# Two-source VectorE operations for the mirrored copies of the first two blocks and for the first step's copy

## Chip, core and metric

The kernel runs on one core of a Trainium2 chip. The metric is the device time of one execution in microseconds (us), from three runs; beside them stands one execution that the hardware profiler recorded. TensorE (PE), VectorE (DVE), ScalarE (ACT) and GpSimd (POOL) compute; the queue of SyncE (SP) and that of ACT issue transfers.

## What is computed

The program is an attention with a complex decaying state, then two feed-forward layers. Only the first part is touched by the change:

```python
B, H, S, D = q.shape                               # 4, 8, 768, 48
mag = np.sqrt(a_re * a_re + a_im * a_im)
scale = np.minimum(mag, 0.999) / (mag + 1e-06)
a_re_n, a_im_n = (a_re * scale, a_im * scale)
for t in range(S):
    ar, ai = (a_re_n[:, :, t, :, None], a_im_n[:, :, t, :, None])
    new_re = ar * S_re - ai * S_im
    new_im = ar * S_im + ai * S_re
    kv = np.einsum('bhd,bhe->bhde', k[:, :, t], v[:, :, t])
    S_re, S_im = (new_re + kv, new_im)
    y[:, :, t] = np.einsum('bhd,bhde->bhe', q[:, :, t], S_re)
```

Behind it, each token goes through one of eight experts (`_moe_ref`) and then through a dense layer with a leaky ReLU (`_moe2_ref`).

## The kernel before

The sequence is cut into chunks of L = 96 steps. Within a chunk the products P of all a up to a step are needed, so that k can be divided and q multiplied by them; these are the rows that `attention_rows` makes. It is called twice, once for each half of the batch. The first call keeps the results in two large tiles called `stash`; the second writes them to memory. A row of its tiles is one of the 128 partitions: two batches, eight heads, eight chunks. The 96 steps are worked off in blocks (BLKA: 4 steps, then ten blocks of 8, then 6, 4 and 2).

For each block i there are these pieces:

- `load_a(i)` brings a_re and a_im of the block into a tile `ari` (three buffers), over the SP queue; `load_kq(i)` brings k and q.
- `norm_pre(i)` is ACT's part of the normalization: squares (`nsq`), logarithm, exponential (`nr`), square (`nrr`). The sum of the two squares is made by PE (`ad`) except in the first three blocks, where DVE makes it.
- `norm(i)` is DVE's part: three operations that end with the factor `rr` (named `nrr` in the rows), then a_re and a_im times `rr` into parts 0 and 2 of the tile `a4` (named `a`). Then parts 3 and 1 get the mirrored copies: part 3 is part 0, and part 1 is minus part 2. In most blocks ACT makes these; in blocks 0 and 1 (MIRROR) DVE does, and in the last ones (MIRROR_G) POOL makes one of them.
- `steps(i)` is the recurrence: for each step one multiplication of the last P with the four parts of a (`t<-P,a`) and one sum (`P<-t`). The first step of all has no last P; there P is a copy of parts 0 and 2.
- `scaled_pre(i)`, `scaled(i)` and `turned(i)` make k/P and q*P (`kr`, `qr`), turn them on PE (`qkps`) and copy them into `stash` on ACT.

In the first call the order of all these on DVE, ACT and PE is written out: `timed` gives every piece a place, and the three engines keep it. POOL and SP are filled in the order in which the program comes to them. Between the pieces stand those of `gate_products` (`gv`, `gtps`, `gps`), which work on v for the later gate. Ahead of the block work POOL is given its constants and, last, two memsets that clear partitions 96 to 127 of the two `stash` tiles (12288 elements each).

After this stage come the chunk products and the routing, then experts and dense layers of the first half, beside which the second call of `attention_rows` runs, and then the same for the second half.

Of the kernel before, what the change touches and what calls it, by code (L numbers as in the profile page):

```python
# [14 lines left out]
ALU = mybir.AluOpType  # L15
# [53 lines left out]
MIRROR = (0, 1)  # L69
# [9 lines left out]
def moe_attention_kernel(ctx, tc, q, k, v, a_re, a_im, w_skip, w_gate, w1, w2, w_in, w_out, out,  # L79
# [15 lines left out]
    V, A, T, G = Engine(nc.vector, "V"), Engine(nc.scalar, "A"), Engine(nc.tensor, "T"), Engine(nc.gpsimd, "G")  # L95
# [58 lines left out]
    def attention_rows(ui, ep, blks, sum_pe, queue, store, stash=None, more=None):  # L154
# [9 lines left out]
        nb = len(blks)  # L164
        tbm = max(blks)

        def rows(src, i):
            return src[b0:b0 + HB].rearrange("b h (c t) d -> c (b h) (t d)", t=L)[
                :, :, t0s[i] * D:(t0s[i] + blks[i]) * D]

        def flat(x):
            return x.rearrange("p t d -> p (t d)")

        def cost(i, n=1):
            return (70 + 1.04 * n * blks[i] * D) / 1e3

        def tl(tag, i, dims=(), after=(), bufs=None):
            kw = {} if bufs is None else {"bufs": bufs}
            t = ep.tile([R, *dims, tbm, *after, D], F32, tag=tag, name=tag, **kw)
            n = blks[i]  # L180
            return t[:, :, :n] if len(dims) == 1 else t[:, :n]

        def both(x, i):
            return x.unsqueeze(2).to_broadcast([R, blks[i], 2, D])
# [14 lines left out]
        def load_a(i):  # L199
            ari = tl("ari", i, (2,), bufs=3)  # L200
            queue.dma_start(flat(ari[:, 0]), rows(a_re, i))
            queue.dma_start(flat(ari[:, 1]), rows(a_im, i))
            ins["a", i] = ari
# [29 lines left out]
        def norm(i):  # L233
            ari = ins.pop(("a", i))
            m2, s2, r0, rr = pre["a", i]
            V.tensor_tensor(rr, m2, rr, ALU.mult)
            yield cost(i)
            V.scalar_tensor_tensor(rr, rr, 3.0, r0, ALU.subtract, ALU.mult)
            yield cost(i)
            V.scalar_tensor_tensor(rr, rr, -2.0, s2, ALU.max, ALU.mult)  # L240
            yield cost(i)
            a4 = tl("a4", i, (), (4,))
            a4s[i] = a4
            if stash:
                V.tensor_tensor(a4[:, :, 0, :], ari[:, 0], rr, ALU.mult)
                yield cost(i)
                V.tensor_tensor(a4[:, :, 2, :], ari[:, 1], rr, ALU.mult)
            else:
                V.tensor_tensor(a4[:, :, 0::2, :], ari.rearrange("p c t d -> p t c d"), both(rr, i), ALU.mult)
            if i + 3 < nb:  # L250
                load_a(i + 3)
            yield cost(i, 2)
            for _ in range(3 if ui else 0):
                yield 0.0
            for c in range(2):
                if stash and i in MIRROR_G and not c:
                    G.tensor_scalar(a4[:, :, 3 - 2 * c, :], a4[:, :, 2 * c, :], 1.0 - 2 * c, None, ALU.mult)
                elif stash and i in MIRROR:
                    V.tensor_scalar(a4[:, :, 3 - 2 * c, :], a4[:, :, 2 * c, :], 1.0 - 2 * c, None, ALU.mult)
                else:  # L260
                    A.activation(a4[:, :, 3 - 2 * c, :], a4[:, :, 2 * c, :], AF.Copy, scale=1.0 - 2 * c)

        def scaled_pre(i):
            P = Ps[i]
            sq = ep.tile([R, tbm, 2, D], F32, tag="psq", name="psq")[:, :blks[i]]
            g0 = tl("pg0", i)
            A.activation(sq, P, AF.Square)
            yield
            n2 = added(sq[:, :, 0, :], sq[:, :, 1, :], i, SUM_SCALED)
            yield  # L270
            s2 = sq[:, :, 1, :]
            A.activation(s2, n2, AF.Ln)
            yield
            A.activation(g0, s2, AF.Exp, scale=-1.0)
            pre["k", i] = n2, g0
# [59 lines left out]
        def steps(i, prev):  # L335
            a4 = a4s.pop(i)
            P = ep.tile([R, tbm, 2, D], F32, tag="P", name="P", bufs=3)[:, :blks[i]]
            Ps[i] = P
            for t in range(blks[i]):
                if prev is None:  # L340
                    V.tensor_copy(P[:, t], a4[:, t, 0::2, :])
                else:
                    t4 = ep.tile([R, 2, 2, D], F32, tag="t4", name="t4", bufs=3)
                    V.tensor_tensor(t4, prev.unsqueeze(1).to_broadcast([R, 2, 2, D]),
                                    a4[:, t].rearrange("p (o i) d -> p o i d", i=2), ALU.mult)
                    yield 0.33
                    V.tensor_tensor(P[:, t], t4[:, :, 0, :], t4[:, :, 1, :], ALU.add)
                prev = P[:, t]
                yield 0.23
# [22 lines left out]
        def timed(more):  # L372
# [18 lines left out]
            at(s0, 1, later(norm_pre, 0), (0, 1, 2, 3, 4))  # L391
            at(s0, 1, later(norm_pre, 1), (4.5, 7.2, 9.5, 10.5, 12.5))
            at(s0, 1, later(norm, 0), (5, 6, 7, 8, 8.5, 9))
            t = end = 0.0
            for i in range(nb + 1):
                t, n = end, max(2.0 * blks[min(i, nb - 1)], LEAST)
                end = t + n
                if i < nb:
                    at(t, 1, later(lambda i: steps(i, Ps[i - 1][:, blks[i - 1] - 1] if i else None), i),
                       range(2 * blks[i] - (i == 0)))  # L400
                if i == nb:
                    at(t, 1, lambda: chunk_products(), (0.5,))
                if i + 1 < nb:
                    at(t, n, later(norm, i + 1), AT_NORM)
                if i + 2 < nb:
                    at(t, n, later(norm_pre, i + 2), AT_NORM_PRE)
                if i:
                    at(t, n, later(scaled_pre, i - 1), AT_SCALED_PRE)
                    at(t, n, later(scaled, i - 1), AT_SCALED)
                if i > 1:  # L410
                    at(t, n, later(lambda i: turns.pop(0), i), AT_TURNED[:2 * -(-blks[i - 2] // 4)])
# [22 lines left out]
        for j in range(2):  # L434
            for _ in norm_pre(j):
                yield 0.4
            if not j:
                yield from norm(0)
        prev = None
        for i in range(nb):  # L440
            before = ([scaled_pre(i - 1)] if i else []) + ([norm_pre(i + 2)] if i + 2 < nb else [])
            others = ([(None, norm(i + 1))] if i + 1 < nb else []) + ([(("k", i - 1), scaled(i - 1))] if i else [])
            yield from weave(steps(i, prev), before, others)
            prev = Ps[i][:, blks[i] - 1]
# [735 lines left out]
    stash = [p.tile([128, NCH, HB * H, L], F32, name="stash") for p in blocks]  # L1180
    ep = tc.alloc_tile_pool(name="rows0", bufs=2, side="right")
    more = []
    gen = attention_rows(0, ep, BLKA, True, nc.sync, rws[0], stash, more)
    next(gen)
    constants()
# [12 lines left out]
    rt = tc.alloc_tile_pool(name="rt", bufs=1, side="right")  # L1198
    ck[0].take(1)
    behind = attention_rows(1, ep, BLKB, False, nc.sync, rws[1])  # L1200

    def place(e, layer):
# [237 lines left out]
```

## Time and profile before

| | us |
|---|---|
| median of three runs | 968.27 |
| lowest, highest | 965.54, 970.45 |
| the profiled execution | 965.6 |
| its span from the first to the last instruction | 963.3 |

Over the span PE is busy 87%, DVE 65%, ACT 54%, POOL 14%. The chain of work that ended last lies 52% on PE, 19% on DVE, 15% in transfers, 10% on ACT.

The stage of the change is the first 165 us. A busy instruction in these records is one that has been started; the time in which a started instruction is held up counts as its own duration. All kernel instructions carry line 91, that of the helper that records them, so they are told apart by the tiles they write and read. The names in the timeline: start in us, duration in us, engine, line, operation, out<-in, size.

### The profile page before, as it was taken

The numbers are of one execution on the slowest core, as the hardware profiler recorded it, in microseconds if no ns is written. First come the engines' busy times: TensorE is split into PE (matmuls) and PEld (weight loads), VectorE is DVE, ScalarE is ACT, GpSimd is POOL, SyncE is SP. The second block draws the span as 40 slices with busy tenths as digits, with TensorE's granted clock in tenths as the row PEclk, the third lists the DMA queues.
The fourth block names the chain that finished last, engine by engine and source line by source line (L and its number), as shares of the span: only waits on it lengthen the run. The fifth ranks groups of instructions, "written<-read, shape, count | busy, mean of one in ns | idle before, by whom it ended". The sixth has DMA issues, their size and how long they took to land.

```text
span 963.3 us, 17827 instructions
## 1 busy us (share of the span) xinstructions
PE 835.0 (87%) x6674; PEld 581.0 (60%) x6674; DVE 628.5 (65%) x1534; ACT 517.9 (54%) x1065; POOL 137.2 (14%) x168
## 2 busy tenths in 40 slices
PE   0488877899569975699999988999999999999997
PEld 0366666899458853344556978945677645546454
DVE  7998796477868678999990456487668262260440
ACT  2578898566445443564751777656557162250430
POOL 9100011212163001100002211141101000000000
PEclk9978798999879988799999999999999999999999
DMA  4265552798848985625436799332857201000000
GB/s 113 70 184 149 149 143 87 201 264 268 272 152 280 318 289 181 222 86 177 145 97 174 196 256 246 107 119 100 266 182 246 79 9 51 17 0 26 9 10 27
DMA packets 126512, 143.61 MB, mean 149 GB/s; under 512 B 34058, under 2 KB 109514, under 8 KB 126416
## 3 DMA queue, kind: packets, MB, share of 16 engines
q1 hardware_dynamic: 106064, 107.88, 38.2%
q10 hardware_dynamic: 18304, 29.89, 9.6%
q0 software_dynamic: 2048, 4.61, 1.4%
q8 instruction: 54, 0.88, 0.4%
q14 instruction: 42, 0.34, 0.1%
HBM read 115.62 MB, written 28.41 MB: 150 GB/s over the span
## 4 chain that ended last, share of the span: by engine, by line
PE 52%; DVE 19%; DMA 15%; ACT 10%; issue 3%; SPq 1%; POOL 0%; ACTq 0%; DVEq 0%; POOLq 0%
PE ops L91 17%; PE hps L91 13%; PE yps L91 7%; PE sps L91 3%; DVE gg L91 3%; DMA raw<-in_moe_w_in_dram 3%; DVE gl L91 3%; DVE cst L91 3%; ACT stash L91 2%; DVE a L91 2%; ACT gh L91 2%; DMA kqt<-kqd 2%; PE tps L91 2%; PE ad L91 2%; DMA vt<-vd 2%
## 5 line engine op out<-in xcount | busy, mean ns | idle before, releaser
L91 PE MATMUL hps<-xTh,m2w 128*128 128x512 f16 x576 | 173.7, 381 | 0.4 <-ACT xTh L91 0.2
L91 PEld LDWEIGHTS <-m2w 128*128 128x128 f16 x864 | 84.4, 98 | 100.3 <-issue 3.2
L91 PE MATMUL ops<-m2w,gh 128*128 128x384 f16 x512 | 125.2, 326 | 0.0
L91 PE MATMUL hps<-xTl,m2w 128*128 128x512 f16 x288 | 109.3, 380 | 0.2 <-DVE xTl L91 0.2
L91 DVE TENSOR_TENSOR gg<-hps,gg 128x512 f32<-128x512 f32 x96 | 65.8, 686 | 65.1 <-ACT gg L91 64.7
L91 PE MATMUL ops<-m2w,gl 128*128 128x384 f16 x256 | 83.6, 327 | 0.0
L91 ACT ACTIVATE ot<-ops 128x384 f32<-128x384 f32 x24 | 11.6, 489 | 121.3 <-PE ops L91 121.3
L91 PEld LDWEIGHTS <-gh 128*128 128x128 f16 x512 | 50.1, 98 | 32.7
L91 DVE TENSOR_TENSOR t<-P,a 128x192 f32<-128x192 f32 x190 | 67.1, 353 | 1.3 <-ACT a L91 0.4
L91 PE MATMUL ops<-m2w,stash 128*128 128x384 f16 x384 | 65.3, 326 | 1.2 <-ACT m2w L91 1.2
L91 DVE TENSOR_TENSOR gl<-gg,gh 128x512 f16<-128x512 f32 x64 | 44.2, 690 | 33.9 <-ACT gh L91 33.2
L91 ACT ACTIVATE gg<-hps 128x512 f32<-128x512 f32 x96 | 56.3, 587 | 17.4 <-PE hps L91 12.0
L91 DVE SCALAR_TENSOR_TENSOR w<-cw,w 128x768 f16<-128x768 f32 x64 | 59.8, 953 | 7.3 <-ACT w L91 7.1
L91 ACT ACTIVATE gh<-gg 128x512 f16<-128x512 f32 x64 | 40.3, 630 | 42.9 <-DVE gg L91 42.7
L91 ACT ACTIVATE w<-cw 128x768 f16<-128x768 f32 x64 | 53.0, 843 | 18.1 <-DMA cw<-in_moe_w_dram 15.7
L91 POOL TENSOR_SCALAR_AFFINE_SELECT sc<-sc 96x384 f32<-96x384 f32 x64 | 35.2, 559 | 156.2 <-ACT sc L91 156.0
L91 PE MATMUL ad<-psq,ident 128*128 128x384 f32 (+2 forms) x48 | 24.9, 657 | 36.8 <-ACT psq L91 36.2
L91 PEld LDWEIGHTS <-stash 128*128 128x128 f16 x384 | 37.5, 98 | 28.6 <-issue 4.3
L91 POOL DMA_INDIRECT xd<-xo,idx x16 | 25.2, 1575 | 179.6 <-DVE xo L91 165.8
L91 ACT ACTIVATE stash<-qkps 96x512 f32<-96x512 f32 (+1 forms) x50 | 50.1, 1026 | 0.3 <-PE qkps L91 0.3
L91 DVE TENSOR_TENSOR P<-t 128x96 f32<-128x96 f32 x190 | 48.1, 253 | 1.6
L91 PE MATMUL yps<-stash,hh 128*128 128x384 f32 x128 | 44.7, 503 | 3.5 <-ACT hh L91 3.5
(245 smaller groups left out, 1786.1 us busy)
## 6 DMA issues: line engine op xcount, KB each, us to landing
stash<-in_moe_w_dram ACTq DMA_DIRECT2D x32, 768.0 KB
cw<-in_moe_w_dram SPq DMA_DIRECT2D x64, 384.0 KB
kqt<-kqd SPq DMA_DIRECT2D x16, 576.0 KB
kqd<-kq SPq DMA_DIRECT2D x14, 576.0 KB
vd<-gv SPq DMA_DIRECT2D x32, 192.0 KB
vt<-vd SPq DMA_DIRECT2D x32, 192.0 KB
raw<-in_moe_w_in_dram SPq DMA_DIRECT2D x16, 384.0 KB
raw<-in_moe_w_out_dram SPq DMA_DIRECT2D x16, 384.0 KB
```

The costliest lines, as they stand in the source:

```text
L91: ins = getattr(self.engine, op)(*args, **kw)
```

## The change

Three edits:

1. In blocks 0 and 1 the mirrored copies are no longer made from parts 0 and 2 by an operation with one source tensor and a constant (`tensor_scalar`), but from `ari` and `rr`, as parts 0 and 2 themselves, by an operation with two source tensors and a constant (`scalar_tensor_tensor`): (a times plus or minus 1) times rr.
2. The first step's P is no longer a copy but the maximum of the same view with itself (`tensor_tensor` with max), again two source operands.
3. Since the mirrored copies now read `ari`, in these two blocks `load_a(i + 3)`, which takes over that buffer, is issued behind them.

```diff
-            if i + 3 < nb:
+            if i + 3 < nb and not (stash and i in MIRROR):
                 load_a(i + 3)
             yield cost(i, 2)
...
                 elif stash and i in MIRROR:
-                    V.tensor_scalar(a4[:, :, 3 - 2 * c, :], a4[:, :, 2 * c, :], 1.0 - 2 * c, None, ALU.mult)
+                    V.scalar_tensor_tensor(a4[:, :, 3 - 2 * c, :], ari[:, c], 1.0 - 2 * c, rr, ALU.mult, ALU.mult)
                 else:
                     A.activation(a4[:, :, 3 - 2 * c, :], a4[:, :, 2 * c, :], AF.Copy, scale=1.0 - 2 * c)
+            if i + 3 < nb and stash and i in MIRROR:
+                load_a(i + 3)
...
                 if prev is None:
-                    V.tensor_copy(P[:, t], a4[:, t, 0::2, :])
+                    V.tensor_tensor(P[:, t], a4[:, t, 0::2, :], a4[:, t, 0::2, :], ALU.max)
```

On DVE, at the start of the program, the operations of block 0 (a_184 is its tile of the four parts; 4x48 its steps and columns) and the first step stand as follows:

```order
 L91 TENSOR_TENSOR nsq<-nsq 128x384
 L91 TENSOR_TENSOR a_184<-ari,nrr 128x4x48 x2
-L91 TENSOR_SCALAR a_184<-a_184 128x4x48 x2
-L91 COPY P<-a_184 128x96
+L91 SCALAR_TENSOR_TENSOR a_184<-ari,nrr 128x4x48 x2
+L91 TENSOR_TENSOR P<-a_184 128x96
 L91 TENSOR_TENSOR nrr<-nsq,nrr 128x384
 L91 SCALAR_TENSOR_TENSOR nrr<-nrr,nr_177 128x384
```

Nothing changes its place; three instructions change their form. The same holds a few instructions on, for block 1 (a_208):

```order
 L91 TENSOR_TENSOR nsq<-nsq 128x384
 L91 TENSOR_TENSOR a_208<-ari,nrr 128x8x48
-L91 TENSOR_TENSOR t_215<-P,a_184 128x192
-L91 TENSOR_SCALAR a_208<-a_208 128x8x48 x2
-L91 TENSOR_TENSOR P<-t_215 128x96
+L91 TENSOR_TENSOR t_212<-P,a_184 128x192
+L91 SCALAR_TENSOR_TENSOR a_208<-ari,nrr 128x8x48 x2
+L91 TENSOR_TENSOR P<-t_212 128x96
```

Here, too, only the form of the two copies changes (the numbers behind t are names). Apart from the first step of the second call (one COPY on DVE, which becomes a TENSOR_TENSOR of the same size), the order on DVE, ACT, PE and POOL is otherwise the same. On SP the loads of a keep their place in the row; further down, two pairs change places. Before:

```order
L481 DMA vd<-gv_149 96x512
L510 DMA vt_0_138<-vd 96x512
L481 DMA vd<-gv_150 96x512
L462 DMA gv_149<-in_v_dram 96x8x48
L207 DMA kq_429<-in_k_dram 128x1x384
L462 DMA gv_150<-in_v_dram 96x8x48
L208 DMA kq_429<-in_q_dram 128x1x384
```

And now:

```order
L483 DMA vd<-gv_149 96x512
L483 DMA vd<-gv_150 96x512
L512 DMA vt_0_138<-vd 96x512
L464 DMA gv_149<-in_v_dram 96x8x48
L464 DMA gv_150<-in_v_dram 96x8x48
L207 DMA kq_429<-in_k_dram 128x1x384
L208 DMA kq_429<-in_q_dram 128x1x384
```

One load of `vt` has moved behind a store of `gv`, and one half of a load of k and q behind a load of v.

## Rows read from the trace of the kernel before

**Rows 1.** Timeline of all engines, 6.4 to 9.2 us: start, duration, operation.

```profile
6.35 10.34 POOL L91 MEMSET stash<- 32x12288 f32 x1
6.53 0.36 ACT L91 ACTIVATE nrr<-nr 128x192 f32<-128x192 f32 x1
...
6.92 0.36 DVE L91 TENSOR_TENSOR nrr<-nsq,nrr 128x192 f32<-128x192 f32 x1 [1.22 <-ACT nrr L91]
...
7.32 0.36 DVE L91 SCALAR_TENSOR_TENSOR nrr<-nrr,nr 128x192 f32<-128x192 f32 x1
...
8.62 0.62 DVE L91 TENSOR_TENSOR a<-ari,nrr 128x192 f32<-128x192 f32 x2
...
9.16 7.64 DVE L91 TENSOR_SCALAR a<-a 128x192 f32<-128x192 f32 x1
```

**Rows 2.** Timeline of all engines, 25 to 110 us: POOL and DVE rows.

```profile
16.63 10.45 POOL L91 MEMSET stash<- 32x12288 f32 x1
16.73 10.47 DVE L91 TENSOR_SCALAR a<-a 128x192 f32<-128x192 f32 x1
27.12 0.19 DVE L91 COPY P<-a 128x96 f32<-128x96 f32 x1
27.23 0.55 DVE L91 TENSOR_TENSOR nrr<-nsq,nrr 128x384 f32<-128x384 f32 x1
...
28.56 0.55 DVE L91 SCALAR_TENSOR_TENSOR nrr<-nrr,nsq 128x384 f32<-128x384 f32 x1
29.02 0.25 DVE L91 TENSOR_TENSOR P<-t 128x96 f32<-128x96 f32 x1
29.19 0.55 DVE L91 TENSOR_TENSOR a<-ari,nrr 128x384 f32<-128x384 f32 x1
29.66 0.55 DVE L91 TENSOR_TENSOR nsq<-nsq 128x384 f32<-128x384 f32 x1
...
30.87 0.62 DVE L91 TENSOR_SCALAR a<-a 128x384 f32<-128x384 f32 x2
...
31.41 0.25 DVE L91 TENSOR_TENSOR P<-t 128x96 f32<-128x96 f32 x1
...
41.22 0.55 DVE L91 TENSOR_TENSOR nrr<-ad,nrr 128x384 f32<-128x384 f32 x1
```

**Rows 3.** Chain of work that ended last, whole span: start, us, what.

```profile
8.62 18.57 DVE a L91 x4
40.74 1.09 PE qkps L91 x4
```

**Rows 4.** Timeline of all engines, 0 to 32 us: ACT and SP rows.

```profile
9.85 0.52 ACT L91 ACTIVATE nrr<-nr 128x384 f32<-128x384 f32 x1
10.28 0.51 ACT L91 ACTIVATE nsq<-nr 128x384 f32<-128x384 f32 x1
...
14.98 0.62 SPq L201 DMA_DIRECT2D ari<-in_a_re_dram  x1
15.65 0.60 SPq L202 DMA_DIRECT2D ari<-in_a_im_dram  x1
...
30.25 0.52 ACT L91 ACTIVATE nsq<-nsq 128x384 f32<-128x384 f32 x1 [17.86 <-DVE nsq L91]
...
30.75 0.60 SPq L201 DMA_DIRECT2D ari<-in_a_re_dram  x1
```

**Rows 5.** Busy time by stretch, us of each engine, granted clock, DMA share, GB/s.

```profile
19.00:19.25 0.25, 0.00 (x0) 0.00 (x0) 0.25 (x1) 0.00 (x0) 0.25 (x1) 1.00 0.09 31
19.25:30.75 11.50, 0.00 (x0) 0.00 (x0) 11.47 (x11) 0.50 (x1) 7.83 (x1) 1.00 0.00 0
```

**Rows 6.** Timeline of ACT, 29 to 52 us.

```profile
32.80 0.83 ACT L91 ACTIVATE nsq<-ari 128x768 f32<-128x768 f32 x1
...
36.98 0.49 ACT L91 ACTIVATE nsq<-ad 128x384 f32<-128x384 f32 x1 [0.18 <-PE ad L91]
...
38.06 0.53 ACT L91 ACTIVATE nrr<-nr 128x384 f32<-128x384 f32 x1
```

**Rows 7.** Timeline of POOL, 100 to 170 us, its first row.

```profile
119.24 0.51 POOL L91 TENSOR_SCALAR nsq<-nr 128x384 f32<-128x384 f32 x1 [92.16 <-ACT nr L91]
```

**Rows 8.** Busy time by stretch: PE, PEld, DVE, ACT, POOL, granted clock, DMA share, GB/s.

```profile
27.00:50.00 23.00, 13.02 (x68) 9.71 (x69) 22.33 (x71) 14.86 (x32) 0.08 (x1) 0.93 0.32 89
50.00:75.00 25.00, 20.65 (x126) 15.74 (x124) 22.66 (x68) 20.37 (x40) 0.00 (x0) 0.78 0.59 169
...
465.00:963.30 498.30, 480.06 (x3888) 310.43 (x3885) 252.66 (x515) 240.99 (x469) 48.06 (x65) 0.99 0.37 111
```

## Prediction

> **What bounds the kernel now.** I read the chain of work that ended last first. Near its start it holds 18.57 us for four DVE operations that write the tile a, of 128x192 elements each [rows 3]. The timeline of the engines shows which ones: the two multiplications of block 0 take 0.62 us together [rows 1], the two mirrored copies 7.64 and 10.47 us [rows 1, 2]. An operation of the same form on twice the elements takes part in a pair of 0.62 us later on [rows 2]. So these are not long operations; they are held up, and the profile books that as busy time. What holds them stands beside them: POOL clears the two stash tiles from 6.35 to 16.69 and from 16.63 to 27.08 us, and the copies end at 16.80 and 27.20, each about 0.1 us behind a memset [rows 1, 2]. No semaphore ties the two engines there; the copies touch other tiles. Not every DVE operation is held: those with two source tensors that ran during the first memset, tensor_tensor as well as scalar_tensor_tensor, took 0.36 us for 192 elements [rows 1]. All that were held have one source.
>
> While DVE is held the others run dry. ACT waits 17.86 us for DVE, and the transfers stand at 0 GB/s from 19.25 to 30.75 us [rows 4, 5]. After 27.23 us DVE is busy 22.33 of 23 us [rows 8]; it sets the pace of this stretch, and what it starts later, all starts later.
>
> **The change part by part.** I write each place as "before" minus "after".
>
> Block 0's copies and the first step. Before, the first copy starts at 9.16 and the operation behind the first step (nrr of block 1) at 27.23 [rows 1, 2]. After, two operations with two sources and 192 elements follow each other as the two multiplications do, which start at 8.62 and leave DVE free for the copy at 9.16: 0.54 us for the pair [rows 1]. The maximum over 96 elements holds DVE as a sum of that size does, 29.02 to 29.19, 0.17 us [rows 2]. DVE would then be at nrr at 9.16 + 0.54 + 0.17 = 9.87 us. But nrr of block 1 needs ACT's square, which ends at 9.85 + 0.52 = 10.37 [rows 4]; with about 0.03 us on the way (6.89 to 6.92) [rows 1], it starts at 10.40. That is what is late next, and it takes 0.53 of the gain. Gain: 27.23 - 10.40 = 16.83 us. ACT's other value for block 1 ends at 10.79 [rows 4]; DVE wants it at 28.56 - 16.83 = 11.73 [rows 2], so it costs nothing.
>
> It has to be all three instructions. A single one left with one source would still wait to about 27.1 us; the diff turns all of them, and the order of DVE shows none with one source among those that follow in the time of the memsets.
>
> Block 1's copies. Before, the pair starts at 30.87 and the next operation at 31.41: 0.54 us [rows 2]. After, each has two sources and 384 elements, and such a one holds DVE from 29.19 to 29.66, 0.47 us [rows 2]; the pair takes 0.94. Loss: 0.40 us, on the path, since DVE has no gap there. Left: 16.43 us. In the second call one copy becomes a maximum of the same size: 0.17 instead of the 0.11 us from 27.12 to 27.23, a loss of 0.06 us, which I leave out.
>
> The loads of a that move. load_a(3) now waits for block 0's copies, which end near 9.8 us. SP is issuing other loads until 14.98 and comes to it then, as before [rows 4]. So the move costs nothing. load_a(4) was issued at 30.75 [rows 4]; after, it waits for block 1's copies, some 16 us earlier in all, and goes out right behind load_a(3). What is queued behind it on SP is loads and stores of v, which go out earlier too. The two swaps further down SP's row concern a load of vt that this stage doesn't read, and half a load of k and q for a block that starts much later: nothing.
>
> The load that gets uncovered. load_a(3) has landed when the transfers stop, between 19.00 and 19.25 us [rows 5]. Before, ACT read it at 32.80 [rows 6], so the stall covered it. After, ACT would want it at 32.80 - 16.43 = 16.37 and gets it about 19.15: ACT stands 2.8 us. From there to what DVE needs of it: ACT's end of that square, PE's sum, and ACT's next read of it at 36.98, then nrr at 38.06 + 0.53 = 38.59 [rows 6], 5.79 us after 32.80. So it is ready at 19.15 + 5.79 = 24.94. DVE wants it at 41.22 - 16.43 = 24.79 [rows 2]. Loss: 0.15 to 0.2 us; the bounds are 0 (PE has less queued ahead of the sum then) and the whole 2.8 us, if ACT never makes the delay good. I take 0.2, near the lower end, since ACT is busy only 14.86 of the 23 us there [rows 8].
>
> POOL. The memsets go on to 27.08 as before, now beside DVE; POOL's next instruction is at 119.24 us after an idle 92 us [rows 7], so even 16 us less leaves it far ahead.
>
> **Sum.** 16.83 - 0.40 - 0.2 = 16.2 us. Against the profiled execution that is 965.6 - 16.2 = 949.4 us (span 963.3 - 16.2 = 947.1). The median lies 2.67 us above the profiled execution; from it, 968.27 - 16.2 = 952.1. All that follows hangs on engines and semaphores and has no fixed hour: the weights' transfers are issued by ACT behind this stage, in program order. So I let the gain pass to the end whole.
>
> **The rivals.**
>
> A: the new operations wait as well, because what counts is that POOL works and DVE reads a second tensor. Then block 0's pair ends at 27.2 as before, and the time is 968.27 + 0.40 + 0.06 = 968.7, no change. For it: the trace shows no mirrored scalar_tensor_tensor beside a memset. Against it: the six others with two sources that ran beside the first memset, four of which stand in the rows [rows 1], show no delay. The Trainium skill reads both ways: "GPSIMD Engine Reference", Key points, has VectorE operations with two SBUF inputs contend with GpSimd without a condition, which is this rival; "SBUF — State Buffer", Who interferes with whom, limits it to a GpSimd instruction that reads SBUF, and a memset only writes. By the second, the trace agrees with its 0.36 us. Chance 0.07.
>
> B: ACT's 2.8 us pass to the end. ACT is busy 20.37 of 25 us after 50 us [rows 8], so it has less room to catch up there. Gain 16.43 - 2.8 = 13.6, time 954.7. Chance 0.12.
>
> C: the stage is really limited by its transfers, and the stall only hid that. Then no more can be won than the hole in them, 11.5 us [rows 5]: 956.8. Against it: the transfers' share is 0.32 and 0.59 in the stretches behind [rows 8]. Chance 0.08.
>
> D, the slower side: TensorE's clock. The last 498.3 us have 480.06 us of PE work at a granted clock of 0.99 [rows 8]. If the earlier start of the stage led into other clock phases and this one fell to 0.94, it would cost 480.06 x (0.99/0.94 - 1) = 25.5 us: 968.27 - 16.2 + 25.5 = 977.6. The gain is gone at 480.06 x (0.99/x - 1) = 16.2, x = 0.958. For it: in other stretches the clock is 0.78 to 0.93 [rows 8]. Against it: PE works without a gap at the end, and nothing is changed there. Chance 0.03.
>
> **How the numbers follow.** Forecast 0.70, A 0.07, B 0.12, C 0.08, D 0.03. About 0.5%, 4.84 us, can be told from no change. Faster: forecast, B and C, 0.90; same: A, 0.07; slower: D, 0.03. The range: at best DVE's own 9.87 us holds and nothing else is lost, 27.23 - 9.87 = 17.4, from the lowest run 965.54: 948.1; the clock of the first stage can give a little more: the 20.65 us of PE work at 0.78 would be 3.3 us less at the 0.93 of the stretch before [rows 8], and PE shares that stage's chain with ACT and DVE, so I grant half, 1.6: 946.5. At worst C from the highest run, 970.45 - 11.5 = 959.0. A and D are left out.
>
> **What would show it.** In the profile after: block 0's copies of a as scalar_tensor_tensor of about 0.36 us each near 9.2 us; nrr of block 1 at 10.4; both memsets still of 10.4 us; ACT's square of load_a(3) waiting for its load at about 19.2; PE's first work some 16 us earlier; the last copies into stash some 16 us earlier; the stretch from 465 us on moved but as long. It is wrong if one of the new operations shows a duration of several us, if DVE waits over 1 us for ACT between 20 and 30 us, or if the stage up to the routing shrinks by 16 and the end does not.

## The result

The changed kernel takes 958.18 us (median of four runs, 956.44 to 958.91) where the kernel before, on the same chip, takes 969.23 (four runs, 965.54 to 970.45). The ratio is 0.9895, with a 95% interval of 0.9864 to 0.9926: faster by more than the 0.5% that can be told apart. The time lies in the forecast range, but 11 us came where the sum says 16.2. One run of the kernel before, on a later chip, took 1823.37 us at a granted clock of 1.00, where all others took 963 to 974 at 0.94 to 0.96; it is left out below. The profiled execution took 956.44 us with a span of 954.0, 9.3 us less than the span before.

### The hold is gone

The timeline of all engines after the change, from 6 us on (start, duration, engine, line, operation, result<-sources, tile, count, and in brackets the idle time before and its releaser), answers to [rows 1, 2]:

```profile
6.34 20.62 POOL L91 MEMSET stash<- 32x12288 f32 x2
...
8.77 0.62 DVE L91 TENSOR_TENSOR a<-ari,nrr 128x192 f32<-128x192 f32 x2
9.31 0.62 DVE L91 SCALAR_TENSOR_TENSOR a<-ari,nrr 128x192 f32<-128x192 f32 x2
9.85 0.25 DVE L91 TENSOR_TENSOR P<-a 128x96 f32<-128x96 f32 x1
...
10.56 0.56 DVE L91 TENSOR_TENSOR nrr<-nsq,nrr 128x384 f32<-128x384 f32 x1 [0.46 <-ACT nrr L91]
...
14.21 1.02 DVE L91 SCALAR_TENSOR_TENSOR a<-ari,nrr 128x384 f32<-128x384 f32 x2
```

POOL's two memsets are as long as before. Beside them the two mirrored copies of block 0 take 0.62 us together, not 7.64 and 10.47 [rows 1, 2]; the first step is made in 0.25 us; and `nrr` of block 1, at 27.23 before [rows 2], starts at 10.56 and waits for ACT only. So DVE is 16.67 us ahead here.

### A new wait, one block on

ACT, PE, DVE and SP (queue of the loads) in the same timeline, 15 to 28 us. Only the rows are shown that bear on the load of block 3:

```profile
15.20 0.63 SPq L201 DMA_DIRECT2D ari<-in_a_re_dram  x1
...
16.12 0.52 ACT L91 ACTIVATE psq<-P 128x384 f32<-128x384 f32 x1 [0.48 <-DVE P L91]
...
20.01 0.84 ACT L91 ACTIVATE nsq<-ari 128x768 f32<-128x768 f32 x1 [3.37 <-DMA ari<-in_a_im_dram]
...
20.91 2.93 PE L91 MATMUL ad<-nsq,ident 128*128 128x384 f32 x4 [2.50 <-ACT nsq L91]
...
23.87 0.49 ACT L91 ACTIVATE nsq<-ad 128x384 f32<-128x384 f32 x1 [1.57 <-PE ad L91]
...
25.50 0.56 DVE L91 TENSOR_TENSOR nrr<-ad,nrr 128x384 f32<-128x384 f32 x1 [0.46 <-ACT nrr L91]
...
26.16 0.83 ACT L91 ACTIVATE psq<-P 128x768 f32<-128x768 f32 x1
...
26.31 1.47 PE L91 MATMUL gps<-w,gvT 112*96 112x18 f32 x8 [1.20 <-ACT gvT L91]
...
27.62 1.07 PE L91 MATMUL qkps<-ident,kr 128*96 128x128 f32 x4
```

ACT stands 3.37 us for `load_a(3)`, and PE 2.50 us behind it. `nrr` of block 3 on DVE is 41.22 - 25.50 = 15.72 us ahead of before [rows 2], but PE's first `qkps` only 40.74 - 27.62 = 13.12 [rows 3]. The chain of work that ended last (start, us, what) goes through the same place. Where it had DVE's four operations on `a` [rows 3], it now has the load, and ACT and PE behind it:

```profile
15.87 4.06 DMA ari<-in_a_im_dram
...
20.01 0.85 ACT nsq L91
...
20.91 2.94 PE ad L91 x4
...
26.31 1.47 PE gps L91 x8
27.78 0.90 PE qkps L91 x4
...
150.96 2.80 PE kps L91 x16
```

The last line is PE's first `kps`, with which the chunk products begin and the stage ends. Before, it started at 164.11 us. So 13.15 us come out of the stage.

Two stretches of the changed kernel, 23 us from 10.6 on and the last 498.3 us (start:end, length, busy us of PE, PEld, DVE, ACT and POOL with their counts, granted clock, DMA share, GB/s), answer to [rows 8]:

```profile
10.60:33.60 23.00, 13.07 (x52) 9.07 (x52) 21.61 (x66) 13.03 (x27) 16.36 (x2) 1.00 0.55 145
...
455.70:954.00 498.30, 479.12 (x3865) 310.54 (x3862) 249.79 (x505) 238.23 (x462) 46.89 (x65) 0.99 0.37 109
```

DVE has 0.7 us less work in its 23 us than before. The end of the program is as it was: the same clock, PE without gaps.

### The profile page after: what moved, and what is told of

Same layout as the page of the kernel before. It is cut to its first block, busy times and chain, and to the rows that moved or that the text cites. A ratio compares the mean times of both kernels' runs of the same rounds, so it can differ in the third digit from the quotient of the medians.

```text
span 954.0 us, 17829 instructions
## 1 busy us (share of the span) xinstructions
PE 840.4 (88%) x6674; PEld 584.8 (61%) x6674; DVE 612.4 (64%) x1534; ACT 518.0 (54%) x1065; POOL 137.2 (14%) x168
## 4 chain that ended last, share of the span: by engine, by line
PE 55%; DVE 16%; DMA 14%; ACT 10%; issue 3%; SPq 1%; ACTq 0%; POOL 0%; DVEq 0%; POOLq 0%
PE ops L91 17%; PE hps L91 13%; PE yps L91 7%; PE sps L91 4%; DVE gg L91 3%; DMA raw<-in_moe_w_in_dram 3%; DVE gl L91 3%; DVE cst L91 2%; PE ad L91 2%; ACT stash L91 2%; PE tps L91 2%; ACT gh L91 2%; DMA kqt<-kqd 2%; PE ups L91 2%; DMA cw<-in_moe_w_dram 2%
## 5 line engine op out<-in xcount | busy, mean ns | idle before, releaser
L91 ACT ACTIVATE hh<-hps 128x256 f32<-128x256 f32 (+1 forms) x64 | 23.8, 378 | 40.6 <-PE hps L91 28.7
```

The costliest lines, as they stand in the source:

```text
L91: ins = getattr(self.engine, op)(*args, **kw)
```

## The experiments

In the tables and sentences below, "lead" is how much earlier than in the kernel before something starts, in the two profiled executions. Each ratio is to the kernel before, timed on the same chip.

### Parts of the change: which operations are held

**The first step left as a copy** (against the changed kernel):

```diff
-                    V.tensor_tensor(P[:, t], a4[:, t, 0::2, :], a4[:, t, 0::2, :], ALU.max)
+                    V.tensor_copy(P[:, t], a4[:, t, 0::2, :])
```

> The changed kernel with the first step's copy left as it was (one source). Theory: such an operation is held until the memset ends that is running when it comes, not until POOL is done. It comes at 9.85 us, so it ends at 16.8 with the first memset; nrr of block 1 starts at 16.9 (10.56 in the changed kernel, 27.23 before). The late load is covered then, and the stage is ahead of the kernel before by 27.23 - 16.9 - 0.4 = 9.9 us: about 959. Rival, as the prediction had it: it is held to 27.1, and nothing is gained, 968 to 969.

Measured: 959.88 us, ratio 0.9893 (0.9857 to 0.9930); lead at the first `kps` 9.19 us. DVE in the timeline:

```profile
9.23 0.62 DVE L91 SCALAR_TENSOR_TENSOR a<-ari,nrr 128x192 f32<-128x192 f32 x2
9.77 6.96 DVE L91 COPY P<-a 128x96 f32<-128x96 f32 x1
10.48 6.26 DVE L91 TENSOR_TENSOR nrr<-nsq,nrr 128x384 f32<-128x384 f32 x1
```

The copy, one source, is held until 16.73, the end of the first memset, not of the second. So a single instruction left costs one memset and not both. The operation behind it, with two sources, is booked as started at 10.48 and ends with it: its 6.26 us are time in a queue.

**Block 1's pair left with one source** (against the changed kernel):

```diff
+                elif stash and i == 1:
+                    V.tensor_scalar(a4[:, :, 3 - 2 * c, :], a4[:, :, 2 * c, :], 1.0 - 2 * c, None, ALU.mult)
                 elif stash and i in MIRROR:
```

> The changed kernel with block 1's pair of mirrored copies left with one source. Theory: the pair comes at 14.2 us; its first ends with the first memset at 16.8, its second with the second memset at 27.1 to 27.2; the next sum starts at 27.2 against 31.41 before, so the stage is ahead by 4.2 us and the time is near 965. Rival: only the first two operations of a stretch are held (or the pair slips through between the two memsets); then it ends by 17.4 and the stage is ahead by 10 us or more, 959 or less.

Measured: 965.57 us, ratio 0.9957 (0.9935 to 0.9978); lead at `kps` 4.08 us. DVE:

```profile
14.03 13.35 DVE L91 TENSOR_SCALAR a<-a 128x384 f32<-128x384 f32 x2
...
28.53 0.55 DVE L91 TENSOR_TENSOR nrr<-nsq,nrr 128x384 f32<-128x384 f32 x1
```

The pair that took 0.62 us behind the memsets [rows 2] takes 13.35 us when it comes while they run, to 27.38. Before, block 1 was never held, because block 0 kept it back until POOL was done. Changed alone, block 0 hands most of its wait on: of the lead 4.08 us are left.

### The cause from POOL's side

**The memsets cut into 16 pieces each**, nothing else (against the kernel before):

```diff
-        G.memset(x[2 * D:].rearrange("p c b t -> p (c b t)"), 0.0)
+        z = x[2 * D:].rearrange("p c b t -> p (c b t)")
+        for j in range(16):
+            G.memset(z[:, 768 * j:768 * (j + 1)], 0.0)
```

> The kernel before, its DVE operations untouched, but each of POOL's two memsets of 12288 elements cut into 16 of 768. Theory: DVE is held by the one instruction on POOL that is running, and gets its turn between two; each of the two copies of block 0 ends within about 0.7 us, nrr of block 1 starts near 10.6 to 11.5 instead of 27.23, and the time falls by about as much as in the changed kernel, to 958 to 959. Rival 1: POOL's next memset always comes first and DVE waits to 27 as before: no change, 969. Rival 2: the copies are held by something else than the memsets: no change.

Measured: 954.4 us, ratio 0.9831 (0.9800 to 0.9862); lead at `kps` 11.25 us. DVE and POOL:

```profile
6.35 22.40 POOL L91 MEMSET stash<- 32x768 f32 x32
...
9.03 1.66 DVE L91 TENSOR_SCALAR a<-a 128x192 f32<-128x192 f32 x2
10.62 0.82 DVE L91 COPY P<-a 128x96 f32<-128x96 f32 x1
10.73 0.71 DVE L91 TENSOR_TENSOR nrr<-nsq,nrr 128x384 f32<-128x384 f32 x1
...
14.55 1.37 DVE L91 TENSOR_SCALAR a<-a 128x384 f32<-128x384 f32 x2
```

No DVE instruction is touched, and the hold shrinks to about one piece for each held operation (22.40/32 = 0.70 us; the two copies take 1.66 us together). In time the gain is 15.2 us, more than the 11 expected, and of the size of the change's. So what holds a one-source operation is the one POOL instruction that is running, and DVE gets its turn when that ends.

**The second memset replaced by a POOL copy of the first stash** (against the changed kernel; it writes the same zeros, but reads SBUF):

```diff
+        G.memset(z[0], 0.0)
+        G.tensor_copy(z[1], z[0])
```

> The changed kernel with POOL's second memset replaced by a copy of the cleared part of the first stash tile to the second: POOL now reads SBUF from 16.7 us on, for 10 us or more. Theory by the rule that a VectorE operation with two SBUF inputs contends with a GpSimd instruction that reads SBUF, and not with one that only writes it: DVE runs free to 16.7 us as in the changed kernel and is then held in one two-source operation until the copy ends, near 27 us, and again with nothing after; the stage is ahead of the kernel before by only 4 to 6 us. Rival: what counts is the one-source form of the DVE operation alone; then nothing is held and the stage is ahead by 13 us as in the changed kernel.

Measured: 954.55 us, a single run, beside 970.38 before. POOL and DVE:

```profile
6.36 10.34 POOL L91 MEMSET stash<- 32x12288 f32 x1
...
13.89 1.02 DVE L91 SCALAR_TENSOR_TENSOR a<-ari,nrr 128x384 f32<-128x384 f32 x2
...
16.76 10.79 POOL L91 COPY stash<-stash 32x12288 f32<-32x12288 f32 x1
17.18 10.58 DVE L91 TENSOR_TENSOR t<-P,a 128x192 f32<-128x192 f32 x1
```

Beside the memset the two-source operations run free. Beside the copy one of the same kind is held for 10.58 us, until 27.76, 0.2 us behind POOL's end. Its lead at `kps` is 8.34 us, more than the 4 to 6 of the theory. So rival A's mechanism exists, but not for a memset. This is the rule of the Trainium skill, "SBUF — State Buffer", Who interferes with whom: a VectorE operation with two inputs in SBUF contends with a GpSimd instruction that reads SBUF, and not with one that only writes it. Both of its halves are in these rows. (The time is still 954.55, although the stage gave 4.8 us less than with the change: the rest of the program took 796.3 us in this run, the shortest in all the traces; how that scatters is shown below.)

### The load that was uncovered

**A fourth buffer for `ari`, and `load_a(3)` issued at the start** (against the changed kernel):

```diff
-            ari = tl("ari", i, (2,), bufs=3)
+            ari = tl("ari", i, (2,), bufs=4 if stash else 3)
...
+        if stash:
+            load_a(3)
...
-            if i + 3 < nb and stash and i in MIRROR:
-                load_a(i + 3)
+            if i + ahead < nb and stash and i in MIRROR:
+                load_a(i + ahead)
```

Here `ahead` is 4 in the first call and 3 in the second, and `load_a(3)` stands behind `load_kq(1)`. Every later load of a in the first call goes out one block earlier, too; but between 20 and 120 us ACT waits for such a load only once in the changed kernel, the 3.37 us shown above.

> The changed kernel with a fourth buffer for a in the first call, so that load_a(3) is issued ahead of the gate weights and of v instead of at 15.2 us. Theory: from 40 us on the changed kernel is only 13.1 us ahead of the kernel before although DVE was 16.3 us ahead at 31 us, because ACT waited 3.4 us for load_a(3) and PE and ACT hand that on. Then ACT squares block 3 at 16.6 to 16.8 us without a wait, the first qkps starts near 24.6 (27.6 in the changed kernel), kps near 148 (150.96), and the time is about 3 us below the changed kernel, near 955. Rival: PE and ACT limit the stage by themselves and would have lost the same; then the wait is gone but kps starts at 150.5 to 151 and the time is that of the changed kernel, 958.

Measured: 950.27 us, ratio 0.9798 (0.9766 to 0.9829). ACT and DVE:

```profile
16.66 0.52 ACT L91 ACTIVATE psq<-P 128x384 f32<-128x384 f32 x1 [0.48 <-DVE P L91]
...
17.09 0.83 ACT L91 ACTIVATE nsq<-ari 128x768 f32<-128x768 f32 x1
...
24.73 0.84 ACT L91 ACTIVATE psq<-P 128x768 f32<-128x768 f32 x1 [0.79 <-DVE P L91]
...
25.50 0.55 DVE L91 TENSOR_TENSOR nrr<-ad,nrr 128x384 f32<-128x384 f32 x1
```

ACT's wait is gone, and `psq` of block 1 comes 1.43 us earlier than with the change (26.16), now waiting for DVE. `nrr` of block 3 comes at 25.50, as with the change; but `nrr` of block 1 came at 11.10 here and not at 10.56, since ACT waited longer for the first loads. Counted from there, the late load costs 0.54 us on this path. The lead at `kps` is 17.41 us instead of 13.15, and the time 5 us below the 955 expected.

**The changed kernel once more, beside a later load.** The later load has four transfers of 144 KB, whose data nothing reads, on SP ahead of `load_a(3)`, behind the first five loads of v (against the changed kernel):

```diff
+        for j in range(4):
+            idle = dram.tile([L, H, D], F32, name=f"idle{j}")
+            nc.sync.dma_start(idle, v[0, :, 0:L, :].rearrange("h t d -> t h d"))
```

> The changed kernel itself once more, beside the kernel before on the same chip, for a second trace and more times. Theory: the first kps starts at 150.5 to 152 again (13 us ahead of before); from the first tps to the last sps of the second half's chunks it takes anything from 91 to 97 us, as in the six traces so far of kernels that are alike there; the median time is 11 to 13 us below the kernel before. Rival: the changed kernel gives back 2 to 4 us in that part of its own accord; then it is again at 95 or more and the median is 9 to 11 us below.

> The changed kernel with four more transfers of 144 KB that nobody reads put on SP ahead of load_a(3): the suspected wait made longer. Theory: load_a(3) goes out some 4 us later, ACT squares block 3 near 24 instead of 20.0 us, and the delay goes through ACT and PE to the end of the stage one to one: first kps near 155 (150.96 in the changed kernel), time 4 us above the changed kernel, 962. Rival: ACT has room to make such a delay good, as the prediction put it; then kps stays at 151 to 152 and the time at 958.

Measured: unaltered 953.72 us, ratio 0.9840 (0.9808 to 0.9873); with the later load 958.73, ratio 0.9897 (0.9859 to 0.9934). ACT's read of that load with the later load:

```profile
16.27 0.52 ACT L91 ACTIVATE psq<-P 128x384 f32<-128x384 f32 x1 [0.48 <-DVE P L91]
...
22.56 0.84 ACT L91 ACTIVATE nsq<-ari 128x768 f32<-128x768 f32 x1 [5.76 <-DMA ari<-in_a_im_dram]
...
28.70 0.83 ACT L91 ACTIVATE psq<-P 128x768 f32<-128x768 f32 x1
```

The load is 2.55 us later than in the first profile of the change (20.01), and `psq` of block 1 2.54 us later (26.16): one to one. At `kps` 154.50 - 150.96 = 3.5 us are lost, 6.2 against the repetition on the same chip (148.29), whose median is 5.0 us lower. ACT makes nothing of this further delay good. The repetition itself lies outside what was expected: its first `kps` is earlier than 150.5 to 152, and its gain, 16.7 us, is above 11 to 13.

**All three once more on one chip.** Here the kernel before ran twice more, and the changed kernel and the one with the early load once more each.

> The kernel before once more, for a second trace. Theory: DVE's two copies are held to 27.2 us again, and what comes behind to the first kps varies by 2 to 3 us with TensorE's granted clock, as it does in the traces of the changed kernel (150.96 and 148.29): kps between 162 and 166.5; the stretch from the first tps to the last sps between 91 and 97. Rival: the kernel before is steady there (164.1 within 0.5) and only the changed one varies.

> The same a third time: kps between 162 and 166.5 by the theory, 163.6 to 164.6 by the rival.

> The changed kernel a third time. Theory: the median is a matter of clock and transfers from run to run and chip to chip; over many runs the gain is that of the stage, 13 to 16 us, so 954 to 957 beside a kernel before at 969 to 970. Rival: the first result, 11 us, is the true one: 958 to 959.

> The changed kernel with load_a(3) issued early once more, beside the changed kernel on the same chip. Theory: ACT's lateness behind load_a(3), 1.8 us on ACT and PE at 35 us, is all there is between the two: 2 to 3 us below the changed kernel. Rival: no difference beyond the noise, within 1 us.

Measured, in us. "Median" is over all runs of the group (one run each for the kernel before again and the third time); the other columns are of the one profiled execution, from the timeline of PE, and "rest" is from the first `kps` to the end of the span, where the code is the same in all but for the first step of the second call:

```
kernel          median   span  first qkps  first kps   rest
before           968.27  963.3      40.74     164.11  799.2
before again     967.27  964.8      40.72     164.39  800.4
before, third    962.74  960.3      40.71     163.72  796.6
changed          958.18  954.0      27.62     150.96  803.0
changed again    953.72  948.7      26.41     148.29  800.4
changed, third   955.99  955.1      26.90     150.37  804.7
early load       950.27  953.9      25.02     146.70  807.2
early, again     951.53  948.4      24.59     148.36  800.0
later load       958.73  957.7      29.56     154.50  803.2
```

Three things stand in it. The kernel before comes to `kps` within 0.7 us each time, as the rival had it, although its clock from 60 to 90 us was 0.77 twice and 0.89 once; the changed kernel spreads over 2.7 us. Then, the last pair on one chip: the changed kernel ratio 0.9860 (0.9826 to 0.9894), with the early load 0.9826 (0.9792 to 0.9861), and in the stage 150.37 - 148.36 = 2.0 us between them (in the median 4.5, where 2 to 3 were expected). Last, the rest lasts 796.6 to 807.2 us; the three executions of the kernel before differ by 3.8 us in it, the two with the early load by 7.2. Its mean is 798.7 us for the kernel before, 802.7 with the change and 803.6 with the early load, so up to 4 us of the gain may be given back there; two or three executions with such a spread can't settle it, and the medians of all runs, next, speak against it.

Over all its measurements the changed kernel has a median of 955.66 (16 runs, 950.51 to 958.91), the kernel before 969.39 (42 runs on four chips), a difference of 13.7 us; its mean lead at `kps` is 14.2. The kernel with the early load has 951.21 (11 runs, 948.10 to 956.27). It is faster than the kernel before by 18.2 us (mean lead 16.6), and than the changed one by 4.4 us. On the last chip, with six runs of each, the early load is faster than the changed kernel by 3.9 us in the mean, with a 95% interval of 1.1 to 6.6: the sign of this last step is shown, its size only roughly.

**Where the lead goes.** From the timelines of DVE and ACT on the last pair, lead in us at DVE's third operation on `nrr` of the block and at ACT's `psq` of the block; the last column is the first `kps`:

```
              block    1      2      3      4    first kps
DVE  changed       16.93  16.53  16.42  15.92   13.74
DVE  early load    16.55  16.14  16.15  16.15   15.75
              block    0      1      2      3
ACT  changed       16.52  15.00  14.49  13.77   13.74
ACT  early load    16.13  16.14  16.15  15.92   15.75
```

With the early load both engines keep about 16.1 us for four blocks. With the change ACT drops to 15.0 at once and to 13.8 two blocks on, and DVE follows it down. DVE's waits in the stage, 20 to 120 us (engine, tile, what it waited for: us in total, times, longest), first the changed kernel, then the one with the early load:

```profile
DVE pu L91 <- ACT pg L91: 12.2, 7, 3.6
```

```profile
DVE pu L91 <- ACT pg L91: 10.4, 6, 2.8
```

In this pair the 1.8 us that DVE waits longer for ACT's `pg` are nearly all of the 2.0 us. From one execution to the next this wait changes as much: in the three profiles of the changed kernel it is 12.3, 8.4 and 12.2 us.

## Why the prediction was right and wrong

**What holds DVE: right.** One-source operations (TENSOR_SCALAR and COPY) are held by POOL's memset, and two-source operations (TENSOR_TENSOR and SCALAR_TENSOR_TENSOR) are not. The change, the cut memsets and the copy on POOL show it from three sides. That a single one left "would still wait to about 27.1 us" was wrong: the first step's copy ended at 16.73. A held operation waits for the POOL instruction that is running, not for POOL to be done. The sum did not use this sentence.

**Block 0 and block 1: right.** The sum has 16.83 us up to `nrr` of block 1 and takes off 0.40 for block 1's pair. Measured are 16.67 and 1.02 - 0.62 = 0.40 us. The 16.43 that this leaves is close to what DVE keeps with the early load, 16.1 to 16.6 us over four blocks.

**"The load that gets uncovered": the step that failed.** The sum takes 0.2 us for it. Measured are 1.5 to 2.0 us at `psq` of block 1 (table below), and 2.0 us at the first `kps` in the pair on one chip, 2.4 when counted from `nrr` of block 1. The first profile shows 16.67 - 13.15 = 3.5 us lost in all behind `nrr` of block 1, 0.4 of them block 1's pair. The load itself was nearly foreseen: ACT waits from 16.64 to 20.01, where the text says 16.37 to 19.15. The path that was followed, from ACT's square over PE's sum to `nrr` on DVE, came out nearly as computed, too: from `nrr` of block 1 to `nrr` of block 3 it is 14.94, 14.63 and 14.50 us in the three profiles of the change, and 14.40 and 14.39 with the early load, so 0.1 to 0.5 us. But the square was followed to one successor only. Behind it on ACT, in a fixed order, stand `gvT` and `psq` of block 1; behind these on PE `gps`, `qkps` and the next sum `ad`; and `pg`, which DVE needs, comes from that. `psq` of blocks 0 and 1 stood here before (timeline of ACT):

```profile
32.37 0.52 ACT L91 ACTIVATE psq<-P 128x384 f32<-128x384 f32 x1
...
40.45 0.84 ACT L91 ACTIVATE psq<-P 128x768 f32<-128x768 f32 x1 [1.07 <-DVE P L91]
```

So it was due at 40.45 - 16.43 = 24.02, and came at 26.16. And "near the lower end, since ACT is busy only 14.86 of the 23 us there" read ACT's idle time as room. How much room there is shows when ACT's starts are counted from its `psq` of block 0 (us, from the timelines of ACT):

```
                      square of block 3   psq of block 1
before, three times                0.43     8.06 to 8.08
early load, twice                  0.43             8.07
cut memsets                        2.63             8.78
changed, third                     3.45             9.60
changed again                      3.57             9.73
changed                            3.89            10.04
later load                         6.29            12.43
```

In every late row `psq` is late by 1.5 us less than the square: with the change 3.89 - 0.43 = 3.46 us become 10.04 - 8.07 = 1.97, with the later load 5.86 become 4.36. That is all the room. While the square is in time, `psq` waits for DVE's P (1.07 us before); with the late load it doesn't wait for DVE any more, and what exceeds 1.5 us passes on one to one. The predicted wait of 2.8 us would have cost 1.3. In the changed kernel ACT is busy only 13.03 of 23 us and still makes up no more, because it is idle while it waits for PE (1.57 us ahead of `nsq<-ad`), which waits for ACT (2.50 and 1.20 us): the delay runs round a ring of engines in written order. Behind `psq` of block 1, up to `kps`, the profiles scatter: the changed kernel loses 1.1, wins 0.9 and loses 1.3 us there, the early load wins 1.7 and loses 0.4. What makes this scatter stays open.

**Rival B: the nearest.** It has ACT's delay pass to the end whole, a gain of 13.6 us and 954.7 us. The three profiles of the changed kernel have 13.15, 15.82 and 13.74 us at the first `kps`; the pooled time is 955.66. But the delay did not pass whole, 1.5 us of it were covered, so that the number fits this well is partly luck: the load also came later than foreseen. Its reason, less room for ACT after 50 us, names only part of it: of the 2.8 us that ACT loses against the kernel before on the last chip (16.52 to 13.77), 1.5 are gone at `psq` of block 1, which stood at 40.45 us before.

**"I let the gain pass to the end whole": right, within what can be told.** The last stretch has the clock and the PE work of before. Over many runs the gain at the end, 13.7 us, is the lead at `kps`, 14.2. In the first measurement 5.15 us are missing from the sum: 3.05 in the stage, and 2.1 in the rest. Between single executions the rest varies by up to 10.6 us, within one kernel by up to 7.2, and I take that, with the lead in the stage, as the reason why the first measurement has 11 us, the second 16.7 and the third 12.6; it is not shown. The first stage of the changed kernel varies, too, and its clock with it. Here are 25 us of it, in the changed kernel first and in its repetition second (columns as above):

```profile
90.00:115.00 25.00, 20.24 (x128) 15.00 (x126) 21.38 (x62) 22.17 (x45) 0.51 (x1) 0.86 0.57 147
```

```profile
90.00:115.00 25.00, 20.04 (x147) 15.33 (x145) 22.27 (x66) 22.91 (x46) 1.54 (x2) 0.95 0.58 150
```

The same kernel gets through 147 matmuls at a granted clock of 0.95, and 128 at 0.86, in the same PE time, and the second came to `kps` 2.7 us earlier. That the clock makes the whole of these 2.7 us was not tested.

**The other rivals.** A did not happen; its mechanism showed only beside the POOL instruction that reads (10.58 us). C, not over 11.5 us because the transfers limit the stage, is excluded by the changed kernel's 13.15 us and the early load's 15.75 and 17.41. D did not happen: 0.99 at the end. POOL did have room, as the text says; its next instruction now waits less, but still far from nothing:

```profile
106.11 0.51 POOL L91 TENSOR_SCALAR nsq<-nr 128x384 f32<-128x384 f32 x1 [79.15 <-DVE kr L91]
```

## What to carry to other kernels

When a stall of one engine goes, look for what the stall had covered, and follow the next late thing to all its successors: not only to the engine that sets the pace, but to every instruction queued behind the waiting one. Idle time of an engine in a ring of written order is not room, since it is idle for the others in the ring; how much room there is, only the starts of the late instruction's successors show, here 1.5 us on an engine that was idle for 10 of 23. And a duration that is twenty times that of the same form elsewhere is a wait: look at what runs beside it and ends just before it. Here the remedy may lie on either side, another form of the held operation or shorter pieces of the one that holds it.

## What the runs showed of the hardware

- The hold lasts one POOL instruction, and DVE gets its turn between two that follow each other at once. Cutting 2 memsets into 32 made POOL's work 22.40 instead of 20.73 us long, and the holds 0.7 to 0.8 instead of up to 10.5 us.
- An operation behind a held one is booked as busy as well: the `nrr` that shows 6.26 us behind the held copy takes 0.56 elsewhere. Durations added up by instruction can thus count one wait twice; the busy time of a stretch does not (6.90 of 6.90 us from 9.8 to 16.7 us).
